# First MLP's y product three steps behind its h product in the first block, third buffer of g, scaled x in raw v's buffers

## Chip, cores, metric

The kernel runs on one core of a Trainium2 chip. The metric is the device time of one execution in microseconds (us). Before the change three runs gave 720.06, 719.28 and 715.47 us, so the median is 719.28 us; the profiled execution took 716.73 us, of which 715.0 us are the span between its first and last instruction.

## What is computed

Windowed attention (with a few global positions) over 2 batches, 8 heads, 768 tokens and 64 columns a head, then two MLPs on the 1536 tokens of 512 columns:

```python
x = attention(q, k, v, n_global, n_local)      # 1536 x 512
h = x @ w_in                                   # 512 -> 2048
x = (h * np.cos(h)) @ w_out                    # 2048 -> 512
g = x @ w_gate                                 # 512 -> 1536
silu = g * (1.0 / (1.0 + np.exp(-g)))
out = (silu * (x @ w_val)) @ w_out2            # 1536 -> 512
```

All operands are float32 (the weights come as wider words and are narrowed on the chip). Each float32 product is made of three matmuls: every operand is split into a rounded high part and a low rest, and high x high, high x low and low x high are summed.

## The kernel before

**Stages.** A prologue does the attention of tiles 0 to 3 (of 128 tokens each; there are 12). Then `first_mlp` walks through 48 steps: 3 blocks of 512 tokens times 16 column blocks j of w_in and w_out. A step s makes `h_mm(s)` (12 matmuls, h = x w_in, L274), the chain of cos on VectorE (DVE) and ScalarE (ACT), and `y_mm` (12 matmuls, y += g w_out, L350). Attention of tiles 4 to 11 is strewn over steps 0 to 30 by the table BASES. From step 32 on, and in `second_mlp`, the order is fixed by hand; before that the instructions of each engine are put in order by a list scheduler that takes the order of the code as priority and puts in the waits for buffers.

**The chain of a step.** `chain_a`: k (ACT, L300) from h. `chain_b`: f (DVE, L311), then sine and square on ACT (L320, L321). `chain_c`: h is overwritten in place by f times h (DVE, L328), and its high part goes into g (ACT, L332). `chain_d`: the low part of g (DVE, L338), which reads h for the last time. h lies in PSUM and has two buffers (pool `hp`, `bufs=2`), so h(s+2) can't start before `chain_d(s)` has ended. g has two buffers, y four PSUM banks, one per 128 output columns. ACT needs a table load when it goes from sine to the exponentials of the attention (L848) or back.

**Weights.** In the first block each w block is fetched (`get`), narrowed by three DVE instructions (`use`: L183, L186, L193) and split for its step (`prep_in`, `prep_out`: ACT L206, then DVE or GpSimd L210, by the tables WIE and WOE). Later blocks only split again.

**Order of the loop.** Step s of the first 32 does `h_mm(s)`, `y_mm(s - 2)`, `prep_in(s + 1)`, `chain_b(s - 1)`, attention, `chain_c(s - 1)`, `chain_d(s - 1)`, narrowing of w_in(s + 2) and w_out(s), `prep_out(s - 1)` and `chain_a(s)`.

**Buffers that the change touches.** Raw v is loaded by SP (L702) into two buffers `vr`; `v_scale_part` (L660) reads them in the prologue and `split_v` (L709 to L718) later. The attention output is scaled by `x_norm` into `xn` (L901, a buffer of its own) and transposed on TensorE (PE, L220). SP's queue holds loads and the DMA transposes pt<-ph (L865) in one order. The output of the last MLP leaves through tiles `osb` (L547, L549).

Of the kernel before, what the change touches and what calls it, by code (L numbers as in the profile page):

```python
# [22 lines left out]
P = 128  # L23
# [30 lines left out]
E4 = 2  # L54
LAG = 2
VB = 5
VBE = 7
# [12 lines left out]
def attention_moe_moe2_kernel(  # L70
# [175 lines left out]
    def first_mlp(c1, before, steps, last_block):  # L246
# [60 lines left out]
        def chain_f(s):  # L307
            n = BLOCKS[todo[s][0]][1]
            h, k = hs[s]
            f = ch_p.tile([P, 512], F32, tag="f", name="f")  # L310
            nc.vector.scalar_tensor_tensor(  # L311
                out=f[:, :n], in0=h[:, :n], scalar=INV2PI, in1=k[:, :n],
                op0=ALU.mult, op1=ALU.subtract,
            )
            fs[s] = f
# [49 lines left out]
        def begin():  # L365
            get("i", 0)
            get("i", 1)
            get("o", 0)
            use("i", w_in, 0)
# [4 lines left out]
        ch_p = c1.enter_context(tc.tile_pool(name="ch", bufs=2))  # L374
        g_p = c1.enter_context(tc.tile_pool(name="g", bufs=2))
        yp = c1.enter_context(tc.tile_pool(name="yp", bufs=4, space=PSUM))
        last = nsteps - NF1
        for s in range(last):
            early, late = steps.get(s, ((), ()))
            if s < NF1:  # L380
                get("i", s + 2)
                get("o", s + 1)
            ps = h_mm(s)
            if s >= 2:
                y_mm(s - 2)
# [8 lines left out]
            if s < NF1:  # L394
                use("i", w_in, s + 2)
                use("o", w_out, s)
            prep_out(s - 1)
            chain_a(s, ps)
# [50 lines left out]
    def second_mlp(c2, ch_p, g_p, hp, yp):  # L449
# [51 lines left out]
        def silu(s):  # L501
            n = BLOCKS[todo[s][0]][1]
            sl = ch_p.tile([P, 512], F32, tag="f", name="sl")
            nc.scalar.activation(out=sl[:, :n], in_=ps_.pop(("g", s))[:, :n], func=AF.Silu)  # L504
# [15 lines left out]
        def o_mm(s):  # L520
# [5 lines left out]
            for m in range(nt // P):  # L526
# [8 lines left out]
                if j == NF2 - 1:  # L535
                    end = b == len(BLOCKS) - 1
                    o = ch_p.tile([P, DM], F32, tag="kf"[end and m // 2], name="osb")
                    rows = slice(t0 + m * P, t0 + (m + 1) * P)
# [56 lines left out]
    def windowed_path():  # L595
# [7 lines left out]
        with ExitStack() as ca:  # L603
# [42 lines left out]
            pt_p = ca.enter_context(tc.tile_pool(name="pt", bufs=4, side="right"))  # L646
            xn_p = ca.enter_context(tc.tile_pool(name="xn", bufs=1, side="right"))
            sm_p = ca.enter_context(tc.tile_pool(name="sm", bufs=2, side="right"))
# [243 lines left out]
            def x_norm(i):  # L892
# [6 lines left out]
                nc.vector.tensor_tensor(out=r, in0=r, in1=vsc[b][:, H:2 * H], op=ALU.mult)  # L899
                xn = xn_p.tile([P, DM], F32, tag="xn", name="xn")  # L900
                nc.vector.tensor_tensor(  # L901
# [300 lines left out]
```

## Time and profile before

| | us |
|---|---|
| median of three runs | 719.28 |
| lowest, highest | 715.47, 720.06 |
| the profiled execution | 716.73 |
| its span | 715.0 |
| PE busy in the span | 662.3 (93%) |
| PE weight load busy | 521.5 (73%) |
| DVE busy | 483.9 (68%) |
| ACT busy | 394.7 (55%) |
| GpSimd busy | 115.3 (16%) |

The profile's times are us from the start of the span. Its shares are means over very different stages: from about 300 us on PE hardly waits, and in the first 200 us DVE is nearly as busy as PE. So each stage has to be read by itself.

### The profile page before, as it was taken

How to read it: one execution, taken by the hardware profiler on the slowest of the kernel's cores; microseconds unless marked ns; L12 is line 12 of the kernel's file. 1: busy time of each engine (PE TensorE's matmuls, PEld its weight loads, DVE VectorE, ACT ScalarE, POOL GpSimd, SP SyncE). 2: the span in 40 equal slices, each digit the busy share in tenths (PEclk: the TensorE clock that was granted, in tenths of full speed). 3: DMA queues.
4: the chain of work that ended last, by engine and by line, in shares of the span. 5: the costliest groups of instructions: out<-in, count | busy, mean ns of one | idle time of the engine just before them, and what ended most of it. 6: DMA issues, size and time to landing. Idle time of an engine off the chain costs nothing.

```text
span 715.0 us, 9068 instructions
## 1 busy us (share of the span) xinstructions
PE 662.3 (93%) x3276; PEld 521.5 (73%) x3276; DVE 483.9 (68%) x886; ACT 394.7 (55%) x820; POOL 115.3 (16%) x108
## 2 busy tenths in 40 slices
PE   4777898987898999999999999999999999999997
PEld 3345676756676777787888888888888888888885
DVE  4795999989987566747999869878443444433442
ACT  5566678777486898766666743332333333333331
POOL 2564333523322332420000000000000000000000
PEclk9996799998999999999999999999999999999999
DMA  6788546648534122300332224542000000100001
GB/s 222 190 195 211 170 132 224 172 130 201 136 104 68 37 49 45 60 1 30 102 104 89 88 59 126 161 126 88 30 30 0 1 1 0 60 0 1 1 0 63
DMA packets 69652, 62.73 MB, mean 88 GB/s; under 512 B 48896, under 2 KB 55296, under 8 KB 69600
## 3 DMA queue, kind: packets, MB, share of 16 engines
q1 hardware_dynamic: 69456, 61.95, 31.4%
q8 instruction: 27, 0.44, 0.2%
q14 instruction: 25, 0.20, 0.1%
q10 hardware_dynamic: 144, 0.13, 0.1%
HBM read 47.19 MB, written 3.15 MB: 70 GB/s over the span
## 4 chain that ended last, share of the span: by engine, by line
PE 65%; DVE 16%; ACT 10%; DMA 4%; issue 2%; POOL 1%; SPq 0%; DVEq 0%; ACTq 0%; POOLq 0%
PE v L492 14%; PE o L528 14%; PE g L492 14%; PE h L274 10%; PE y L350 10%; DMA pt<-ph 3%; ACT sb L848 3%; DVE w L193 2%; DVE w L186 2%; DVE sb L830 1%; PE s L778 1%; DVE w L183 1%; ACT L320 1%; ACT L848 1%; DVE h L328 1%
## 5 line engine op out<-in xcount | busy, mean ns | idle before, releaser
L210 DVE TENSOR_TENSOR ws<-w,ws 128x512 fp32r<-128x512 f32 x161 | 112.6, 720 | 95.1 <-ACT ws L206 94.9
L350 PE MATMUL y<-g,ws 128*128 128x512 f32 x576 | 145.8, 399 | 12.9 <-ACT g L332 11.4
L274 PE MATMUL h<-xh,ws 128*128 128x512 f32 (+1 forms) x392 | 136.3, 409 | 3.9 <-ACT xh L225 2.2
L350 PEld LDWEIGHTS y<-g,ws 128*128 128x128 f32 x576 | 109.1, 191 | 39.2 <-ACT g L332 10.9
L206 ACT CAST ws<-w 128x512 fp32r<-128x512 f32 x204 | 121.9, 615 | 21.1 <-DVE w L193 13.3
L528 PE MATMUL o<-ws,a 128*128 128x512 f32 x432 | 104.7, 391 | 0.0
L492 PE MATMUL v<-xh,ws 128*128 128x512 f32 x288 | 96.3, 395 | 0.0
L274 PEld LDWEIGHTS h<-xh,ws 128*128 128x128 f32 x392 | 77.4, 200 | 24.5 <-DVE g L338 3.6
L492 PE MATMUL g<-xh,ws 128*128 128x512 f32 x288 | 94.7, 390 | 0.0
L528 PEld LDWEIGHTS o<-ws,a 128*128 128x128 f32 x432 | 81.1, 188 | 18.4
L274 PE MATMUL h<-xl,ws 128*128 128x512 f32 (+1 forms) x196 | 78.8, 402 | 0.0
L210 POOL TENSOR_TENSOR ws<-w,ws 128x512 fp32r<-128x512 f32 x43 | 60.3, 1403 | 109.6 <-ACT ws L206 98.6
L504 ACT ACTIVATE sl<-g 128x512 f32<-128x512 f32 x36 | 21.5, 598 | 97.5 <-PE g L492 97.5
L492 PEld LDWEIGHTS v<-xh,ws 128*128 128x128 f32 x288 | 54.2, 188 | 12.7
L514 ACT CAST a<-sl 128x512 fp32r<-128x512 f32 x36 | 22.4, 622 | 72.6 <-DVE sl L510 72.6
L492 PEld LDWEIGHTS g<-xh,ws 128*128 128x128 f32 x288 | 54.1, 188 | 11.2
L492 PE MATMUL v<-xl,ws 128*128 128x512 f32 x144 | 56.9, 395 | 0.0
L492 PE MATMUL g<-xl,ws 128*128 128x512 f32 x144 | 56.0, 389 | 0.0
L193 DVE SCALAR_TENSOR_TENSOR w<-st,w 128x512 int32<-128x512 int32 x68 | 53.9, 802 | 0.8
L186 DVE SCALAR_TENSOR_TENSOR w<-st,w 128x512 int32<-128x512 int32 x68 | 48.6, 723 | 1.2
L300 ACT ACTIVATE k<-h 128x512 int32<-128x512 f32 x48 | 28.4, 592 | 34.4 <-PE h L274 34.3
L311 DVE SCALAR_TENSOR_TENSOR f<-h,k 128x512 f32<-128x512 f32 x48 | 32.9, 685 | 20.8 <-ACT k L300 20.5
(111 smaller groups left out, 821.9 us busy)
## 6 DMA issues: line engine op xcount, KB each, us to landing
st<-w1i SPq DMA_DIRECT2D x16, 512.0 KB, 3.8
st<-w1o SPq DMA_DIRECT2D x16, 512.0 KB, 4.3
st<-w2g SPq DMA_DIRECT2D x12, 512.0 KB, 3.7
st<-w2v SPq DMA_DIRECT2D x12, 512.0 KB, 3.7
st<-w2o SPq DMA_DIRECT2D x12, 512.0 KB, 3.7
vr<-v SPq DMA_DIRECT2D x16, 256.0 KB, 3.8
kr<-kT SPq DMA_DIRECT2D x12, 256.0 KB, 4.1
qr<-qT SPq DMA_DIRECT2D x12, 256.0 KB, 3.4
```

Of the source, the lines that this page charges most:

```text
L186: nc.vector.scalar_tensor_tensor(out=w, in0=hi, scalar=-(1 << 30), in1=w, op0=ALU.bitwise_and, op1=ALU.bitwise_or,)
L193: nc.vector.scalar_tensor_tensor(out=w, in0=lo, scalar=29, in1=w, op0=ALU.logical_shift_right, op1=ALU.bitwise_or,)
L206: nc.scalar.copy(out=s[:, 0, :], in_=w)
L210: e.tensor_tensor(out=s[:, 1, :], in0=w, in1=f32(s[:, 0, :]), op=ALU.subtract)
L274: nc.tensor.matmul(hps[s][:, c0:c1], lhsT=wis[s][:, a, k * P:(k + 1) * P], rhs=xx[:, k, t0 + c0:t0 + c1], start=(k == 0 and a == 0 and xx ...
L300: nc.scalar.activation(out=k[:, :n], in_=ps[:, :n], func=AF.Copy, scale=INV2PI)
L311: nc.vector.scalar_tensor_tensor(out=f[:, :n], in0=h[:, :n], scalar=INV2PI, in1=k[:, :n], op0=ALU.mult, op1=ALU.subtract,)
L350: nc.tensor.matmul(ys[b][m][:, :n], lhsT=w[:, a, m * P:(m + 1) * P], rhs=g[:, c, :n], start=(j == 0 and a == 0 and c == 0), stop=(j == NF1 ...
L492: nc.tensor.matmul(ps[:, :n], lhsT=w[:, a, k * P:(k + 1) * P], rhs=xx[:, k, t0:t0 + n], start=(k == 0 and a == 0 and xx is xh), stop=(k == ...
L514: nc.scalar.copy(out=a[:, 0, :n], in_=sl[:, :n])
L528: nc.tensor.matmul(os_[b][m], lhsT=a[:, c, m * P:(m + 1) * P], rhs=w[:, d, :], start=(j == 0 and c == 0 and d == 0), stop=(j == NF2 - 1 an ...
L848: nc.scalar.activation(out=a, in_=a, func=AF.Exp, bias=nm[:, h:h + 1], accum_out=sm[:, h:h + 1])
```

## The change

In the first 20 steps `y_mm` runs three steps behind `h_mm` instead of two; step 20 (`CATCH`) does two y products, and after it the distance is two again. The fetch, narrowing and split of w_out move one step later with it. g gets a third buffer. Room for it comes from f, which goes from two buffers to one, and from `xn`, which loses its own buffer and takes one of the two of `vr`. The second MLP's silu tile moves from f's buffers to k's, and three of the four output tiles of a block leave through g's buffers, the fourth through f's.

```diff
+CATCH = 20
-            f = ch_p.tile([P, 512], F32, tag="f", name="f")
+            f = ch_p.tile([P, 512], F32, tag="f", bufs=1, name="f")
...
-            get("o", 0)
...
-        g_p = c1.enter_context(tc.tile_pool(name="g", bufs=2))
+        g_p = c1.enter_context(tc.tile_pool(name="g", bufs=3))
...
                 get("i", s + 2)
-                get("o", s + 1)
+                get("o", s)
+            elif s == NF1:
+                get("o", s - 1)
             ps = h_mm(s)
-            if s >= 2:
+            if s <= CATCH:
+                if s >= 3:
+                    y_mm(s - 3)
+            if s >= CATCH:
                 y_mm(s - 2)
...
                 use("i", w_in, s + 2)
-                use("o", w_out, s)
-            prep_out(s - 1)
+                if s >= 1:
+                    use("o", w_out, s - 1)
+            elif s == NF1:
+                use("o", w_out, s - 1)
+            if s < CATCH:
+                prep_out(s - 2)
+            if s >= CATCH - 1:
+                prep_out(s - 1)
...
-            sl = ch_p.tile([P, 512], F32, tag="f", name="sl")
+            sl = ch_p.tile([P, 512], F32, tag="k", name="sl")
...
-                    o = ch_p.tile([P, DM], F32, tag="kf"[end and m // 2], name="osb")
+                    if m < 3:
+                        o = f32(g_p.tile([P, 2, DM], F32R, tag="g", name="osb")[:, 0, :])
+                    else:
+                        o = ch_p.tile([P, DM], F32, tag="f", bufs=1, name="osb")
...
-                xn = xn_p.tile([P, DM], F32, tag="xn", name="xn")
+                xn = vr_p.tile([P, DM], F32, tag="vr", name="xn")
```

The scheduler makes a new order of the first 250 us from this. Three places follow. Lines of the changed kernel are 1 higher near the top (L274 is L275) and 13 higher in the attention (L848 is L861).

PE, from the end of tile 6's attention product (x) to h of step 12. Before, the first four matmuls of y(10) (one for each of y's four banks, with g's high part) stand there:

```order
L888 MATMUL x_1780<-vs_1734,pt_1710 128x64
L350 MATMUL y_942<-g_1787,ws_1799 128x512
L350 MATMUL y_943<-g_1787,ws_1799 128x512
L350 MATMUL y_944<-g_1787,ws_1799 128x512
L350 MATMUL y_945<-g_1787,ws_1799 128x512
L274 MATMUL h_1836<-xh_106,ws_1773 128x512
L274 MATMUL h_1836<-xl_107,ws_1773 128x512
```

In the changed kernel the whole of y(9) and two transposes stand there:

```order
L901 MATMUL x_1756<-vs_1710,pt_1686 128x64
L351 MATMUL y_981<-g_1690,ws_1775 128x512 x3
L351 MATMUL y_982<-g_1690,ws_1775 128x512 x3
L351 MATMUL y_983<-g_1690,ws_1775 128x512 x3
L351 MATMUL y_984<-g_1690,ws_1775 128x512 x3
L221 MATMUL xT_1877<-ident_124,xn_1875 128x128 x2
L275 MATMUL h_1812<-xh_106,ws_1749 128x512
```

So y(10) has gone behind h(12), and what stands ahead of h(12) is a product of the step before it.

ACT, at the first exponentials of tile 8, around step 14. Before, these stand after the sine of step 14, all behind one table load:

```order
L225 CAST xh_106<-xT_2101 128x4x128
L332 CAST g_2144<-h_2037 128x512
L848 ACT_TABLE_LOAD
L848 ACTIVATE sb_1977,sum_1973<-sb_1977,nm_1972 128x256 x2
L848 ACTIVATE sb_2075,sum_1973<-sb_2075,nm_1972 128x256 x2
L300 ACTIVATE k_2155<-h_2110 128x512
```

In the changed kernel the sine of step 14 (f_2116) stands between two of them:

```order
L226 CAST xh_106<-xT_2077 128x4x128
L861 ACT_TABLE_LOAD
L861 ACTIVATE sb_1953,sum_1949<-sb_1953,nm_1948 128x256 x2
L321 ACT_TABLE_LOAD
L321 ACTIVATE f_2116<-f_2116 128x512
L861 ACT_TABLE_LOAD
L861 ACTIVATE sb_2051,sum_1949<-sb_2051,nm_1948 128x256
```

There are two table loads more here, and 25 instead of 23 in the whole program.

SP's queue in the prologue, at the transposes of tile 2. Before, the loads of raw v of the second batch (vr_666, vr_671 are its last two) stand behind them:

```order
L865 DMA_TRANSPOSE pt_594<-ph_591 128x8x128
L865 DMA_TRANSPOSE pt_599<-ph_596 128x8x128
L702 DMA vr_666<-v 128x512
L702 DMA vr_671<-v 128x512
L110 DMA kr_76<-kT 128x4x128
L865 DMA_TRANSPOSE pt_688<-ph_685 128x8x128
```

In the changed kernel one load (vr_577) stands between these transposes, and two more ahead of the first of tile 3 (pt_683):

```order
L878 DMA_TRANSPOSE pt_589<-ph_586 128x8x128
L715 DMA vr_577<-v 128x512
L878 DMA_TRANSPOSE pt_594<-ph_591 128x8x128
L111 DMA kr_76<-kT 128x4x128
L715 DMA vr_661<-v 128x512
L715 DMA vr_666<-v 128x512
L878 DMA_TRANSPOSE pt_683<-ph_680 128x8x128
```

A load has moved into the queue ahead of transposes, and its buffer is one that the transposed xn of tile 1 has held.

## Rows read from the trace of the kernel before

**Rows 1.** Page, the clock granted to PE in 40 slices, tenths of full speed

```profile
PEclk9996799998999999999999999999999999999999
```

**Rows 2.** Windows: stretch, length, busy time of each engine, clock, DMA share, GB/s

```profile
60.00:120.00 60.00, 50.23 (x286) 36.97 (x286) 54.25 (x109) 44.24 (x94) 18.70 (x14) 0.87 0.63 181
120.00:180.00 60.00, 51.73 (x268) 39.50 (x268) 54.07 (x112) 46.48 (x106) 23.99 (x20) 0.90 0.65 172
180.00:240.00 60.00, 55.00 (x324) 42.21 (x324) 46.12 (x103) 42.97 (x94) 17.24 (x13) 1.00 0.37 88
240.00:300.00 60.00, 57.95 (x374) 44.72 (x374) 41.55 (x89) 51.37 (x109) 21.00 (x17) 1.00 0.28 54
406.00:715.00 309.00, 303.64 (x1322) 248.07 (x1320) 163.36 (x259) 107.72 (x193) 0.00 (x0) 1.00 0.14 44
```

**Rows 3.** Waits, 60 to 300 us, PE's: total us, times, longest

```profile
PE y L350 <- ACT g L332: 11.4, 7, 4.2
PE x L888 <- DMA pt<-ph: 4.6, 3, 2.4
PE s L755 <- DVE xn L901: 3.3, 2, 2.9
PE h L274 <- DVE g L338: 1.6, 2, 1.1
```

**Rows 4.** Timeline at y(4) and h(6): start, duration, engine, instruction, idle before

```profile
117.98 1.49 PE L350 MATMUL y<-g,ws 128*128 128x512 f32 x4 [3.10 <-ACT g L332]
118.18 0.68 DVE L338 TENSOR_TENSOR g<-h,g 128x512 fp32r<-128x512 f32 x1
119.26 0.63 PE L274 MATMUL h<-xh,ws 128*128 128x512 f32 x1
```

**Rows 5.** Timeline at y(10) and h(12)

```profile
172.06 2.08 PE L350 MATMUL y<-g,ws 128*128 128x512 f32 x4 [4.25 <-ACT g L332]
172.51 0.68 DVE L338 TENSOR_TENSOR g<-h,g 128x512 fp32r<-128x512 f32 x1
173.94 0.63 PE L274 MATMUL h<-xh,ws 128*128 128x512 f32 x1
```

**Rows 6.** Groups of DVE instructions of the weights, 60 to 200 us: busy, mean ns

```profile
L193 DVE SCALAR_TENSOR_TENSOR w<-st,w 128x512 int32<-128x512 int32 x27 | 25.7, 975 | 0.0
L186 DVE SCALAR_TENSOR_TENSOR w<-st,w 128x512 int32<-128x512 int32 x27 | 19.3, 737 | 0.0
L183 DVE TENSOR_SCALAR w<-st 128x512 int32<-128x512 int32 x28 | 15.3, 576 | 3.5 <-DMA st<-w1i 3.5
L210 DVE TENSOR_TENSOR ws<-w,ws 128x512 fp32r<-128x512 f32 x11 | 9.6, 870 | 0.5 <-ACT ws L206 0.4
```

**Rows 7.** Chain that ended last, one whole y product at full clock

```profile
296.36 2.72 PE y L350 x12
```

**Rows 8.** Timeline of ACT around a table load

```profile
108.59 0.62 ACT L206 CAST ws<-w 128x512 fp32r<-128x512 f32 x1 [2.31 <-DVE nm L838]
109.23 1.28 ACT L848 ACT_TABLE_LOAD   x1
110.52 0.51 ACT L848 ACTIVATE sb<-sb,nm 128x256 f32<-128x256 f32 x1
```

**Rows 9.** Page, DMA issues: KB each, us from issue to landing

```profile
vr<-v SPq DMA_DIRECT2D x16, 256.0 KB, 3.8
```

**Rows 10.** Timelines of the prologue: raw v, its absolute value, xT of tile 1, exponentials

```profile
39.96 2.34 SPq L702 DMA_DIRECT2D vr<-v  x2
47.83 0.63 ACT L660 ACTIVATE va<-vr 128x512 fp32r<-128x512 f32 x1 [1.00 <-PE vsum L661]
50.40 0.64 PE L220 MATMUL xT<-ident,xn 128*128 128x128 f32 x4
54.37 0.47 ACT L810 ACTIVATE sb<-s,nm 128x256 f32<-128x256 f32 x1 [1.93 <-DVE nm L800]
```

**Rows 11.** Timeline of the end

```profile
704.01 5.63 PE L528 MATMUL o<-ws,a 128*128 128x512 f32 x24
709.00 0.69 DVE L547 COPY osb<-o 128x512 f32<-128x512 f32 x1 [0.67 <-PE o L528]
709.68 0.42 DVE L541 COPY osb<-o 128x256 f32<-128x256 f32 x1
710.59 0.37 ACTq L544 DMA_DIRECT2D out<-osb  x1
```

More of the change, by code (lines that the diff above doesn't have):

```diff
@@ L646, in windowed_path @@
             pt_p = ca.enter_context(tc.tile_pool(name="pt", bufs=4, side="right"))
-            xn_p = ca.enter_context(tc.tile_pool(name="xn", bufs=1, side="right"))
             sm_p = ca.enter_context(tc.tile_pool(name="sm", bufs=2, side="right"))
```

## The prediction

> **What bounds the kernel now.** I read the windows first, because one share for the whole span says little here. They show where PE can gain at all [rows 2]: from 406 us to the end it is busy 303.64 of 309 us, and the order of its instructions is the same there before and after the change. Nothing is to be had there. Between 60 and 300 us PE is busy 50.23, 51.73, 55.00 and 57.95 of 60 us, so 25.1 us are idle. In the first two of these windows DVE is busier than PE: 54.25 and 54.07 of 60, that is 90%.
>
> The waits of PE come next [rows 3]. The largest is the one that the change speaks of: y's first matmul waits for g's high part, 11.4 us in 7 places. Waits for transposed probabilities (4.6) and for xn (3.3) follow, and h waiting for g's low part has only 1.6. Read alone, this says that y should go one step later.
>
> Then I looked into the timeline at the two longest of the seven, which hold 3.10 and 4.25 of the 11.4 us [rows 4, 5]. The reader should look at what stands behind y on PE: h(s+2), whose PSUM buffer is free only when chain_d(s) has read h(s) for the last time. At y(4) that instruction ends at 118.18 + 0.68 = 118.86, and h(6) starts at 119.26. At y(10) it ends at 173.19, and h(12) starts at 173.94. So h would have waited for the same chain, 0.40 and 0.75 us less long than it did. The chain h, k, f, sine, square, h, g on ACT and DVE is what is late, and y only stands first in the row of those that wait. h keeps its two buffers, so the chain keeps its rate.
>
> **The change part by part.** The sum is made against the profiled execution, 716.73 us, of which 715.0 are the span.
>
> *y behind h.* Where y's first four matmuls stood ahead of h and waited, they now stand behind it, and h starts as soon as its own buffer is free. Gain: 0.40 + 0.75 = 1.15 [rows 4, 5]; for the five shorter waits I take nothing. Between 0 (the chain itself moves) and 11.4 us (all waits vanish and h never takes their place [rows 3]), I take **-1.2**.
>
> *w_out one step later.* In the 16 steps of the first block one w_out less has been narrowed and split by DVE at any time: 0.576 + 0.737 + 0.975 us for the narrowing, and for the split 0.87 us where DVE does it, about every second time early on [rows 6], in sum 2.7 us. This work doesn't vanish, it lies behind step 15, where DVE has room (46.12 of 60 [rows 2]). In the stage that it leaves DVE is 90% busy; with 90% of it on the path it brings **-2.4** (between 0 and -2.7). Its DMA also goes a step later in SP's queue, with no one waiting for it.
>
> *Two y products in step 20.* One y product, 12 matmuls of 2.72 us together [rows 7], leaves steps 3 to 19 and comes back in step 20. Ahead of it PE can come to an h up to 2.72 us earlier wherever PE and not the chain was late; at step 20 it pays that back, with 120 - 112.95 = 7.05 us of idle PE between 180 and 300 us to pay from [rows 2]. I take **0**, between -2.7 and +2.7.
>
> *Third g buffer, one f buffer.* f is written by DVE (L311) and last read by DVE (L328), in that order for successive steps, so one buffer adds no wait on DVE. No wait of g for a y product is among the waits, so the third buffer frees nothing by itself; it only lets y be later. **0**.
>
> *Order on ACT.* The new order has two more table loads, at step 14. Each takes 1.28 us, and the next activation starts at once after it, 109.23 + 1.28 = 110.51 against 110.52 [rows 8]. Two are 2.56 us. Between 180 and 240 us ACT is busy 42.97 of 60, between 240 and 300 us 51.37 [rows 2]; the chain needs it. I take half, **+1.3**, between 0 and 2.6.
>
> The Trainium skill, ScalarE: Activation LUTs, section on what ACT_TABLE_LOAD costs, gives 1283 ns for the load, as here, and 1380 ns more for a drain, 2.66 us in all. The trace shows no drain: the cast ahead ends at 109.21 and the load starts at 109.23 [rows 8]. By the page the two would be an estimated 5.3 us and my half 2.7.
>
> *xn in vr's buffers.* Now a load of raw v must wait for transposes of xn, and xn for the last reader of raw v. In the prologue vr_577 can't be issued before xT of tile 1 has ended at 51.04; before the change two such loads went out between 39.96 and 42.30 [rows 10]. With 3.8 us to land [rows 9] it is there at 54.8, and ACT's order has its absolute value, 0.63 us, ahead of the exponentials that started at 54.37. They would start at 55.5, 1.1 us later. Behind that load in SP's queue stands one transpose of tile 2, and behind ACT's wait stand the exponentials of tile 3. Against that, ACT's later reads of raw v no longer stand where they stood. I take half, **+0.5**, between 0 and, if the same happens again at each of a few later loads, the 7.9 us that PE's waits for pt and xn amount to now [rows 3].
>
> *The end.* The third output tile of the last block takes the buffer of g that the last product reads, so its copy on DVE waits for that product's end. Now it starts at 709.00, while the product runs to 704.01 + 5.63 = 709.64; then it would take 0.69 us, and the half tile behind it on DVE (now from 709.68), ACT's half and the last DMA (now at 710.59) follow that much later [rows 11]. **+0.7**, nothing hides it. At the ends of the other two blocks the same wait costs nothing, since PE goes on with g and v products and isn't waiting for that copy.
>
> Sum: -1.2 - 2.4 + 0 + 0 + 1.3 + 0.5 + 0.7 = -1.1 us, so 715.6 for an execution like the profiled one. That one lay 2.55 us under the median of the three runs; the mean of the four times is 717.9. I put the forecast on that mean: 717.9 - 1.1 = **716.8 us**.
>
> **Rivals.**
> *The waits really go* (faster). If a late chain were a matter of PE's order, with h(s+2) no longer bound to chain_d(s) after the shift, the 11.4 us of y's waits go, and the end costs 0.7: 716.73 - 11.4 + 0.7 = 706.0 us. For it: the granted clock is 0.87 and 0.90 in the two windows where most of the waits lie and 1.00 after [rows 1, 2], so the idle time costs more than itself, and h at the lower clock is longer. Against it: h(6) and h(12) start within 0.75 us of the end of their chains. Chance 0.18. The Trainium skill, TensorE: Matmul & The Clock Gate, in its part on oscillation, tells the same of waits that come again and again: PE is throttled after each, and work that goes on without such gaps runs at the full clock. The trace agrees so far that the lower clock falls in the windows with the most idle time.
>
> *v loads block SP's queue* (slower). A load whose buffer is held by xn stands at the head of SP's queue with the transposes of the next probabilities behind it; x waits for these, and xn for x. From the point on where such a load stands there longer than the 3.8 us of its landing, PE's waits for pt and xn double: 716.73 + 7.9 + 1.1 + 0.7 = 726.4 us. For it: after the change, loads stand between transposes in the queue. Against it: in the steps, a v load is issued four steps ahead of its split. Chance 0.13.
>
> *It does not do what it says.* At h(12) y(9) stands ahead of h, not y(8): the scheduler has undone one step of the distance. If the shift brings nothing and its costs stay: 716.73 + 1.3 + 0.5 + 0.7 = 719.2 us. Chance 0.17.
>
> **How the numbers follow.** The sum as worked out has 0.52. Its own range, with the bounds of w_out, step 20, ACT and the sharing and some 2 us for the scatter between runs (715.47 to 720.06), is 712 to 722. For 8 in 10 the range goes towards both rivals: **709 to 724**. One per cent, 7.2 us, is about what a measurement of this kernel can tell from no change. Within it lie the sum and the case without effect, 0.69; faster 0.18; slower 0.13.
>
> **What would show it.** PE's wait of y for g falls below 3 us and that of h for g's low part rises to 6 us or more; if both are small, the first rival holds. PE's idle time between 60 and 300 us stays between 20 and 28 us, and DVE's share from 60 to 180 us near 90%. h(12) starts within 1 us of the end of chain_d(10). The last DMA goes out about 0.9 us after the last product's end now and 1.6 us then. Waits of PE for pt or xn above 12 us would show the second rival. My prediction is wrong if the chain itself becomes shorter because DVE or ACT gets other instructions ahead of it.

## The result, and the profile after

| | before | after |
|---|---|---|
| median, us | 717.96 (715.47 to 720.06, 4 runs) | 707.63 (707.17 to 708.74, 4 runs) |
| the profiled execution | 716.73, span 715.0 | 708.01, span 705.8 |
| ratio after to before | | 0.9874, 95% interval 0.9851 to 0.9896 |

The change saves 1.3%. The forecast was 716.8 us and its range 709.0 to 724.0, so the time lies 9 us under the one and 1.4 us under the other.

The windows of the changed kernel, with the columns of [rows 2]:

```profile
60.00:120.00 60.00, 51.16 (x286) 38.39 (x287) 55.11 (x120) 49.16 (x101) 21.00 (x17) 0.89 0.73 201
120.00:180.00 60.00, 53.74 (x323) 40.52 (x322) 55.30 (x112) 43.06 (x100) 21.88 (x19) 0.94 0.58 155
180.00:240.00 60.00, 55.08 (x284) 42.29 (x284) 44.92 (x105) 50.70 (x107) 18.30 (x15) 1.00 0.38 92
240.00:300.00 60.00, 57.85 (x389) 45.82 (x386) 38.52 (x80) 48.92 (x103) 20.62 (x16) 1.00 0.24 46
396.80:705.80 309.00, 302.72 (x1318) 247.32 (x1316) 163.38 (x259) 107.08 (x191) 0.00 (x0) 1.00 0.13 43
```

They differ little from [rows 2]. PE is idle for 240 - 51.16 - 53.74 - 55.08 - 57.85 = 22.2 us between 60 and 300 us, where it was 25.1, and DVE is as busy as before. Equal windows hide the gain, because the same 60 us now hold later steps. The waits of PE between 60 and 300 us, to lay beside [rows 3]:

```profile
PE h L275 <- DVE g L339: 6.9, 6, 1.7
PE y L351 <- DVE ws L211: 3.6, 2, 2.6
PE s L768 <- DVE xn L914: 2.7, 2, 1.9
PE y L351 <- ACT ws L207: 2.1, 3, 1.1
PE x L901 <- DMA pt<-ph: 1.9, 2, 1.2
PE y L351 <- ACT g L333: 1.1, 2, 0.9
```

y's wait for g fell from 11.4 to 1.1 us, h's wait for the chain rose from 1.6 to 6.9, and y now also waits for the split of w_out (3.6 + 2.1). The first two the prediction had said; the wait for the split it had not.

To see where the time went, one needs the same event in both kernels, not the same moment. I take `chain_a`'s k<-h on ACT, of which there is one per step. Steps 4, 6 and 8 of the kernel before:

```profile
103.96 0.61 ACT L300 ACTIVATE k<-h 128x512 int32<-128x512 f32 x1
...
123.54 0.60 ACT L300 ACTIVATE k<-h 128x512 int32<-128x512 f32 x1 [0.63 <-PE h L274]
...
140.38 0.57 ACT L300 ACTIVATE k<-h 128x512 int32<-128x512 f32 x1
```

The same steps of the changed kernel:

```profile
101.12 0.58 ACT L301 ACTIVATE k<-h 128x512 int32<-128x512 f32 x1
...
114.22 0.58 ACT L301 ACTIVATE k<-h 128x512 int32<-128x512 f32 x1
...
129.67 0.58 ACT L301 ACTIVATE k<-h 128x512 int32<-128x512 f32 x1
```

From k(4) to k(8) it took 36.42 us and takes 28.55. The table does this for the whole span and for every kernel of this study: the start of k(0), the lengths of four groups of steps, and the stretch from k(31) to the end of the span. All are differences of such rows in the profiled executions. A profiled execution is one run, not the median of its kernel: that of e1 lies 1.8 us above its median, those of e3, e4 and e8 lie 2.7, 2.4 and 4.0 us below theirs.

| profiled kernel | k(0) at | steps 0-4 | 4-8 | 8-17 | 17-31 | k(31) to end | span |
|---|---|---|---|---|---|---|---|
| before | 75.32 | 28.63 | 36.42 | 78.30 | 96.07 | 400.25 | 715.0 |
| before, again (e5) | 73.33 | 28.21 | 36.79 | 77.53 | 99.02 | 400.41 | 715.3 |
| changed | 71.64 | 29.48 | 28.55 | 79.68 | 95.30 | 401.15 | 705.8 |
| e1 sharing alone | 71.47 | 25.15 | 37.22 | 76.59 | 97.61 | 400.56 | 708.6 |
| e2 buffers, old loop | 70.57 | 27.14 | 38.15 | 75.71 | 98.91 | 401.32 | 711.8 |
| e3 y late, w_out early | 70.84 | 27.63 | 37.64 | 76.70 | 96.33 | 401.36 | 710.5 |
| e4 y early, w_out late | 71.56 | 28.73 | 36.16 | 77.46 | 99.17 | 401.42 | 714.5 |
| e6 sharing, three buffers | 77.32 | 26.53 | 38.38 | 75.50 | 97.36 | 400.51 | 715.6 |
| e7 changed, own xn | 73.73 | 30.15 | 30.22 | 79.82 | 95.22 | 401.36 | 710.5 |
| e8 w_out late alone | 73.32 | 33.78 | 38.07 | 77.65 | 96.01 | 400.56 | 719.4 |
| e9 v loaded later | 74.68 | 25.78 | 37.20 | 75.98 | 97.55 | 400.52 | 711.7 |
| e10 changed, tail undone | 72.96 | 29.57 | 29.48 | 78.24 | 95.27 | 400.19 | 705.7 |
| e11 changed, catch at 28 | 71.14 | 29.48 | 29.39 | 78.60 | 96.74 | 401.26 | 706.6 |
| e12 v split on POOL | 73.45 | 28.15 | 40.41 | 73.73 | 97.59 | 400.37 | 713.7 |
| e13 changed, v on POOL | 68.03 | 32.85 | 30.19 | 80.45 | 95.30 | 400.67 | 707.5 |

Against the mean of the two profiles of before, the changed kernel gains 2.7 us ahead of k(0) and 8.1 in steps 4 to 8, loses 1.1 and 1.8 in the groups beside these, gains 2.2 in steps 17 to 31, and loses 0.8 at the end. What happens in steps 4 to 8 is seen in one window, k(4) to k(8). Before:

```profile
103.96:140.38 36.42, 32.03 (x186) 24.47 (x185) 34.69 (x75) 28.65 (x62) 15.44 (x11) 0.95 0.66 185
```

After:

```profile
101.12:129.67 28.55, 26.33 (x168) 19.59 (x166) 27.97 (x59) 25.78 (x57) 13.11 (x10) 1.00 0.62 178
```

DVE is busy 34.69 of 36.42 and 27.97 of 28.55 us: it sets the pace in both, and after the change it has 16 instructions less to do between the same two points. Which ones the groups of DVE in this stretch tell. Before (busy us, mean ns):

```profile
L193 DVE SCALAR_TENSOR_TENSOR w<-st,w 128x512 int32<-128x512 int32 x10 | 9.0, 912 | 0.0
L186 DVE SCALAR_TENSOR_TENSOR w<-st,w 128x512 int32<-128x512 int32 x10 | 7.1, 726 | 0.0
L183 DVE TENSOR_SCALAR w<-st 128x512 int32<-128x512 int32 x9 | 3.6, 417 | 1.0 <-DMA st<-w1i 1.0
```

After:

```profile
L187 DVE SCALAR_TENSOR_TENSOR w<-st,w 128x512 int32<-128x512 int32 x7 | 4.9, 720 | 0.0
L194 DVE SCALAR_TENSOR_TENSOR w<-st,w 128x512 int32<-128x512 int32 x7 | 4.6, 680 | 0.0
L184 DVE TENSOR_SCALAR w<-st 128x512 int32<-128x512 int32 x6 | 4.5, 793 | 0.3 <-DMA st<-w1i 0.3
```

Seven weights are narrowed in these four steps instead of ten: 19.7 us of DVE became 14.0. The clock granted to PE in the stretch rose from 0.95 to 1.00, and its matmuls fell from 186 to 168; ACT's busy time fell from 28.65 to 25.78 us. So other work than the narrowing left these steps as well.

Not all of this is work put off. A weight takes three narrowing instructions, and the 32 weights take 96. Counted from the start of the span, 60 of them stand before k(8) in both profiles of before and 57 in the changed kernel; before k(4) it is 33 and 38. So by k(8) one weight less has been narrowed, and the rest of the difference between k(4) and k(8) was done earlier, ahead of k(4). In sum DVE is busy for 106.9 us up to k(8), where it was 113.7 and 112.0.

### The profile page after: what moved, and what is told of

It reads as the page before. It is cut to its first block, busy times and chain, and to the rows that moved or that the text cites. A ratio compares the mean times of both kernels' runs of the same rounds, so it can differ in the third digit from the quotient of the medians.

```text
span 705.8 us, 9077 instructions
## 1 busy us (share of the span) xinstructions
PE 656.9 (93%) x3276; PEld 517.7 (73%) x3276; DVE 479.5 (68%) x886; ACT 398.0 (56%) x822; POOL 112.6 (16%) x108
## 4 chain that ended last, share of the span: by engine, by line
PE 68%; DVE 14%; ACT 9%; DMA 5%; issue 2%; POOL 1%; SPq 0%; DVEq 0%; POOLq 0%; ACTq 0%
PE v L503 14%; PE o L539 14%; PE g L503 14%; PE h L275 11%; PE y L351 10%; DMA pt<-ph 2%; ACT sb L861 2%; DMA st<-w1i 2%; DVE w L194 2%; DVE w L187 2%; PE s L791 2%; DVE sb L843 1%; DVE ws L211 1%; DVE w L184 1%; PE s L768 1%
## 5 line engine op out<-in xcount | busy, mean ns | idle before, releaser
L211 DVE TENSOR_TENSOR ws<-w,ws 128x512 fp32r<-128x512 f32 x161 | 113.7, 727 | 98.5 <-ACT ws L207 98.4
L275 PE MATMUL h<-xh,ws 128*128 128x512 f32 (+1 forms) x392 | 132.2, 399 | 7.0 <-DVE g L339 6.9
L275 PEld LDWEIGHTS h<-xh,ws 128*128 128x128 f32 x392 | 75.2, 193 | 27.1 <-DVE g L339 9.9
L275 PE MATMUL h<-xl,ws 128*128 128x512 f32 (+1 forms) x196 | 77.0, 393 | 0.0
L211 POOL TENSOR_TENSOR ws<-w,ws 128x512 fp32r<-128x512 f32 x43 | 57.7, 1344 | 119.7 <-ACT ws L207 113.8
L187 DVE SCALAR_TENSOR_TENSOR w<-st,w 128x512 int32<-128x512 int32 x68 | 50.1, 747 | 1.2
L194 DVE SCALAR_TENSOR_TENSOR w<-st,w 128x512 int32<-128x512 int32 x68 | 49.6, 739 | 0.8
L329 DVE SCALAR_TENSOR_TENSOR h<-f,h 128x512 f32<-128x512 f32 x48 | 33.1, 690 | 21.4 <-ACT f L322 21.4
L301 ACT ACTIVATE k<-h 128x512 int32<-128x512 f32 x48 | 28.4, 591 | 29.9 <-PE h L275 29.8
```

The source lines that it names most:

```text
L187: nc.vector.scalar_tensor_tensor(out=w, in0=hi, scalar=-(1 << 30), in1=w, op0=ALU.bitwise_and, op1=ALU.bitwise_or,)
L194: nc.vector.scalar_tensor_tensor(out=w, in0=lo, scalar=29, in1=w, op0=ALU.logical_shift_right, op1=ALU.bitwise_or,)
L211: e.tensor_tensor(out=s[:, 1, :], in0=w, in1=f32(s[:, 0, :]), op=ALU.subtract)
L275: nc.tensor.matmul(hps[s][:, c0:c1], lhsT=wis[s][:, a, k * P:(k + 1) * P], rhs=xx[:, k, t0 + c0:t0 + c1], start=(k == 0 and a == 0 and xx ...
L301: nc.scalar.activation(out=k[:, :n], in_=ps[:, :n], func=AF.Copy, scale=INV2PI)
L329: nc.vector.scalar_tensor_tensor(out=h[:, :n], in0=f[:, :n], scalar=0.5, in1=h[:, :n], op0=ALU.subtract, op1=ALU.mult,)
```

## The experiments

All ratios are to the kernel before in the same comparison (its medians lay between 716.88 and 717.86 us).

| | median, us | ratio, 95% interval |
|---|---|---|
| e1 sharing alone | 708.62 | 0.9875 (0.9836 to 0.9913) |
| e2 buffers, old loop | 713.54 | 0.9953 (0.9921 to 0.9984) |
| e3 y late, w_out early | 715.10 | 0.9963 (0.9938 to 0.9988) |
| e4 y early, w_out late | 718.62 | 1.0019 (0.9994 to 1.0044) |
| e5 before again | 717.07 | one run |
| e6 sharing, three buffers | 718.82 | 1.0022 (0.9984 to 1.0060) |
| e7 changed, own xn | 713.63 | 0.9953 (0.9927 to 0.9978) |
| e8 w_out late alone | 725.26 | 1.0121 (1.0065 to 1.0178) |
| e9 v loaded later | 714.55 | 0.9960 (0.9944 to 0.9976) |
| e10 changed, tail undone | 707.85 | 0.9861 (0.9835 to 0.9888) |
| e11 changed, catch at 28 | 708.74 | 0.9882 (0.9857 to 0.9907) |
| e12 v split on POOL | 715.66 | 0.9969 (0.9953 to 0.9984) |
| e13 changed, v on POOL | 709.53 | 0.9880 (0.9854 to 0.9905) |

My first theory was that the gain ahead of k(0) comes from the sharing, and the gain in the steps from the later y and the relief of DVE by w_out; the rival was that the sharing has no part in it.

**e1, sharing alone.** The kernel before with two edits:

```diff
-            xn_p = ca.enter_context(tc.tile_pool(name="xn", bufs=1, side="right"))
...
-                xn = xn_p.tile([P, DM], F32, tag="xn", name="xn")
+                xn = vr_p.tile([P, DM], F32, tag="vr", name="xn")
```

> The kernel before with one edit: scaled x takes raw v's buffers. In the changed kernel h(0) starts 3.8 us earlier than before, h(6) 8.7 us, and the end 9.2 us. Theory P (the sharing gives the part ahead of h(0)): h(0) 3 to 4 us earlier, the steps as before, 714 us. Theory L (all comes from the later y and w_out; the part ahead of h(0) from w_out 0 no longer loaded and narrowed there): h(0) within 0.5 us of before, 718 us. My recorded term for this edit was +0.5 us: 718.5 us.

708.6 us: neither theory. This edit alone gives nearly the whole gain of the change. The table shows it by another road: 2.9 us ahead of k(0), 3.3 in steps 0 to 4, nothing in steps 4 to 8 and 1.3 in steps 8 to 17. ACT's order has changed too: it has 19 table loads instead of 23, three instead of five both in steps 0 to 4 and in steps 4 to 8.

**e2, the buffers without the later y and w_out.** The changed kernel with the loop of before (`y_mm(s - 2)` throughout, `get("o", 0)` in `begin`, `get("o", s + 1)`, `use("o", w_out, s)`, `prep_out(s - 1)`):

```diff
-            if s <= CATCH:
-                if s >= 3:
-                    y_mm(s - 3)
-            if s >= CATCH:
+            if s >= 2:
                 y_mm(s - 2)
```

> The changed kernel with the loop of the kernel before: y two steps behind h, w_out loaded, narrowed and split when it was; all buffers as changed (third g, one f, xn in vr, output tiles in g). Theory P: the part ahead of h(0) is kept, 3.8 us, the steps as before, 0.7 to 0.9 us lost at the end: 715 us. Theory L: nothing is left but the end's loss, 718.5 us. If the buffers were the whole gain: 708 us.

713.5 us, near theory P's 715, but 4.9 us slower than e1: the third g, the single f and the output tiles in g, which I had put at nothing but the end's 0.7, take more than half of the sharing's gain away again. The order of e2 has 23 table loads again, as before; which of these edits does it was not tried. The end costs 0.8 of it (401.32 against 400.56); steps 0 to 4 take 2.0 us longer than in e1 and steps 17 to 31 take 1.3 longer.

**e3 and e4, one half of the shift each.** e3 is the changed kernel with w_out loaded (the first one in `begin`), narrowed and split as early as before, y three steps late. e4 has y two steps behind, w_out loaded and narrowed one step later:

```diff
 (e3)
-                get("o", s)
+                get("o", s + 1)
...
-                if s >= 1:
-                    use("o", w_out, s - 1)
+                use("o", w_out, s)
...
-            if s < CATCH:
-                prep_out(s - 2)
-            if s >= CATCH - 1:
-                prep_out(s - 1)
+            prep_out(s - 1)
 (e4)
-            if s <= CATCH:
-                if s >= 3:
-                    y_mm(s - 3)
-            if s >= CATCH:
+            if s >= 2:
                 y_mm(s - 2)
...
-            if s < CATCH:
-                prep_out(s - 2)
-            if s >= CATCH - 1:
-                prep_out(s - 1)
+            prep_out(s - 1)
```

> The changed kernel with w_out loaded, narrowed and split in the steps in which it was before, y three steps behind h. Theory Y (the distance of y itself brings the gain in the steps): within 1 us of the changed kernel, 708 us. Theory W (DVE's relief by one w_out less at any time brings it): the gain in the steps, about 5 us, is lost: 713 us, 711 if my recorded 2.4 us for it was right.

> The changed kernel with y two steps behind h throughout, w_out loaded and narrowed one step later as changed (its split in the same step, where y needs it next). Theory W: 708 to 710 us. Theory Y: the gain in the steps is lost, 713 us, and PE's wait of y for g is again 8 to 11 us between 60 and 300 us.

With e2 and the changed kernel this is a square: neither 713.5, y late 715.1, w_out late 718.6, both 707.6 us. Neither theory Y nor W holds. w_out late alone costs 5 us; y late alone gains nothing (the 1.6 us that it lies above e2 can't be told from scatter, and its order has 27 table loads, four more than e2's, so it isn't the distance of y alone); both together gain 6 us. Steps 4 to 8 show where the halves fail: 38.15, 37.64 and 36.16 us without one or the other, 28.55 with both. The narrowing does too: before k(8) stand 60, 60 and 61 of its instructions in e2, e3 and e4, and 57 in all five kernels that have both. In e3 PE's wait of y for g is still there between 60 and 300 us:

```profile
PE y L351 <- ACT g L333: 6.9, 6, 2.3
```

y is later in the program but not in time. The split of w_out(s - 1) needs one of two buffers, and y(s - 3) reads it; with the split as early as before, y(s - 3) has to be out of the way as early as before. (That this is what holds it is read from the code and the wait, it was not tried with a third buffer.) In e4 y's waits for g are back (9.0 us between 60 and 300 us, as theory Y had it), the weights are wanted as early as before, and DVE narrows about ten of them between k(4) and k(8):

```profile
L187 DVE SCALAR_TENSOR_TENSOR w<-st,w 128x512 int32<-128x512 int32 x10 | 7.0, 716 | 0.0
```

**e8, w_out later alone, all buffers as before.** The kernel before with

```diff
-            get("o", 0)
...
-                get("o", s + 1)
+                get("o", s)
...
-                use("o", w_out, s)
+                if s >= 1:
+                    use("o", w_out, s - 1)
+            elif s == NF1:
+                use("o", w_out, s - 1)
```

> The kernel before with w_out loaded and narrowed one step later, split in the step in which it is narrowed; y two steps behind h, all buffers as before. By my recorded term 716.9 - 2.4 = 714.5 us. By the pair with and without this among kernels with the changed buffers (718.6 against 713.5) it costs 5 us: 722 us, with PE's y waiting for the split of w_out or ACT standing in front of it.

725.3 us, a loss of 8 where my term for this part was a gain of 2.4. Steps 0 to 4 take 33.78 us instead of 28.4. Moved later in the program without its reader, the narrowing isn't put off: 62 of its instructions stand before k(8), where 60 stood. I read this as the same deadline with less time.

**e5, before again; e6, sharing with three buffers.** e5 has no edit. e6 is e1 with one more:

```diff
-            vr_p = ca.enter_context(tc.tile_pool(name="vr", bufs=2, side="right"))
+            vr_p = ca.enter_context(tc.tile_pool(name="vr", bufs=3, side="right"))
```

> The kernel before, unchanged, profiled a second time. In the first profile PE's four s products from 16.85 us take 0.29 us each, in all five profiles with sharing 0.18 us from 17.5 us on, although the instructions ahead of them are the same in the same order. Theory C (chance of the clock: the half-rate stretch from 16.85 us is a property of that execution): here the first xn starts near 34.8 us instead of 36.53 and h(0) some 1.7 us earlier, with the rest of the time unchanged. Theory P (the part ahead of h(0) is the sharing's): xn at 36.5 and the first k at 75.3 us again.

> The kernel before with scaled x in raw v's pool, but with three buffers there instead of two, so that as much room is there as before the change. Theory P1 (the shortage, loads of v held back by xn, brings the gain): 716 to 717 us. Theory P2 (the other order that comes with one pool brings it, the shortage nothing): 708 to 710 us, as with sharing alone (708.6).

e5 has k(0) at 73.33 us instead of 75.32 with the same instructions, and the span is 0.3 us longer: theory C holds for about 2 us ahead of k(0), and these 2 us don't reach the end (17 to 31: 99.02 against 96.07). So a part of what one profile shows at the start is chance. A part isn't: in the eight profiles with two shared buffers k(0) lies between 68.0 and 73.0 us, in the six with xn apart between 73.3 and 75.3, on the mean 71.0 against 74.0. The clock granted to PE differs between these executions (from 35 to 65 us 0.94 in e13, which has the earliest k(0), and 0.61 in e10, which has the latest of the eight), so I compare those with 0.71 to 0.77: k(0) lies between 70.6 and 71.6 in five with two shared buffers (changed, e1, e2, e4, e11) and between 73.3 and 74.7 in four with xn apart (e7, e8, e9, e12). With three shared buffers it is 77.3, at a granted clock of 0.60, and the median of the total is 718.8 us, with the widest scatter of all (713.7 to 723.6). So P1 comes out within 2 us of its number: without the shortage there is no gain.

**e7, the change without the sharing.** Room for xn's own buffer comes from k:

```diff
+            xn_p = ca.enter_context(tc.tile_pool(name="xn", bufs=1, side="right"))
...
-            k = ch_p.tile([P, 512], I32, tag="k", name="k")
+            k = ch_p.tile([P, 512], I32, tag="k", bufs=1, name="k")
...
-            sl = ch_p.tile([P, 512], F32, tag="k", name="sl")
+            sl = ch_p.tile([P, 512], F32, tag="kf"[s % 2], bufs=1, name="sl")
```

> The changed kernel with a buffer of its own for scaled x again; the room comes from k, which has one buffer instead of two (the next k is written after f has read the last). If the later y and w_out gain by themselves and the sharing by itself: 707.6 + 4 = 712 us. If the later y and w_out gain nothing without the sharing: 718 us, with the end's 0.9 us. If the sharing gives nothing here: 708 us.

713.6 us. So the later y and w_out do gain without the sharing, 3.4 us, and the sharing gains 6 on top of them (8.3 alone, so the two don't add up: 3.4 + 8.3 would be 11.7, and it is 9 to 10). The 6 us include whatever the lost buffer of k costs e7, which was not tried alone. Between k(4) and k(8) e7 looks like the changed kernel:

```profile
103.88:134.10 30.22, 27.86 (x173) 20.88 (x172) 27.94 (x65) 27.67 (x60) 12.88 (x9) 1.00 0.63 162
```

Here DVE has 27.94 us of work, as in the changed kernel, where e1 has 36.70 in 37.23:

```profile
96.61:133.84 37.23, 33.15 (x190) 25.52 (x188) 36.70 (x81) 26.53 (x62) 14.96 (x11) 0.91 0.66 185
```

The short steps 4 to 8 (28.6 to 30.2 us in all five kernels with y and w_out both late, 36.2 to 40.4 in all ten others) are thus the work of the shift. The sharing counts at the start, where the changed kernel is 2.1 us ahead of e7; alone it also counts in steps 0 to 4.

**e9 and e12, what the sharing does in the steps.** The second block's v come in tiles 4, 5, 6 and so on, each split into two halves. In the order of DVE's instructions before, tile 4's halves stand ahead of f(0), tile 5's between f(0) and f(1), tile 6's between f(4) and f(5). With sharing alone tile 4's stand behind f(0), tile 5's second half behind f(4), tile 6's behind f(5) and f(7). The second theory: v's preparation is held back out of steps that DVE limits. e9 gets the same places in the kernel before by another means, xn keeping its buffer. e12 takes tile 4's halves off DVE, upon which tile 6's stand behind f(5). (The two expectations speak of the first v of the block where the halves that matter are those of tiles 5 and 6.)

```diff
 (e9)
-                add(0, E, load_v, i)
+                add(2, E, load_v, i)
 (e12)
-VLE = "DGGGDDDGDDGD"
+VLE = "DGGGGDDGDDGD"
-VHE = "DDDDDDDDGDDD"
+VHE = "DDDDGDDDGDDD"
```

> The kernel before with one edit: each raw v of the steps is loaded one step later in the program (the last step's half, two half steps later); xn keeps its own buffer. In the order the split of the first v of the second block then stands behind f of step 4, as it does with sharing alone, where before it stood behind f of step 0. Theory V (sharing gains because v's preparation is held back out of steps 0 to 4, where DVE sets the pace): 709 to 712 us, and DVE has spent some 3 us less on v before k of step 6. Theory S (it is the sharing itself, through the part ahead of h(0)): 716 to 717 us. If holding it back costs, because x waits for v: 720 us.

> The kernel before with one edit: the two halves of the first v of the second block are made on POOL (both were on DVE); buffers, loads, y and w_out as before. The order up to the first steps stays that of before. In both profiles of before, the two of this v on DVE stand ahead of f(5), and from k(4) to k(6) it takes 20.0 and 19.6 us; in the kernels where v is held back 16.0 to 16.5. Theory V (the split ahead of f(5) is what lengthens these two steps): k(4) to k(6) in 16 to 17 us, the start as before, and of the 3.5 us up to 4 come back in steps 6 to 10, as with the later load: 713 to 716 us. Theory S (nothing without the sharing): 717 us and 19.6 to 20 us from k(4) to k(6).

e9: 714.6 us, 2.9 us faster by the ratio, more than nothing and less than 709 to 712. Its steps 0 to 4 take 25.78 us, like e1's 25.15: the later place of v in the program is enough to give those steps their gain. Its k(0) is at 74.68, without e1's 2.9 us at the start. That the gain is v's work out of DVE's way, as the theory says, isn't shown. DVE's work on v and on the row maxima of the attention between k(0) and k(4), before:

```profile
L717 DVE CAST vs<-vr 128x512 f16<-128x512 f32 x1 | 0.4, 415 | 0.0
L718 DVE TENSOR_TENSOR vs<-vr,vs 128x512 f16<-128x512 f32 x1 | 0.7, 686 | 0.0
L830 DVE CUSTOM_DVE_ANT_0 sb<-s,m 128x256 f32<-128x256 f32 x8 | 3.0, 415 | 0.0
```

And in e9:

```profile
L717 DVE CAST vs<-vr 128x512 f16<-128x512 f32 x2 | 1.6, 838 | 0.0
L718 DVE TENSOR_TENSOR vs<-vr,vs 128x512 f16<-128x512 f32 x1 | 0.7, 677 | 0.0
L830 DVE CUSTOM_DVE_ANT_0 sb<-s,m 128x256 f32<-128x256 f32 x6 | 2.3, 414 | 0.0
```

DVE is busy 24.85 us there instead of 27.97, but v takes more of it and not less, because tile 4's halves have come in behind f(0); what has gone is other work, two of eight row maxima for one. Like e1, e9 has 19 table loads instead of 23, which is 4 x 1.28 = 5.1 us of ACT. e6 and e12, with 21, have three in steps 0 to 4 and five in steps 4 to 8, and neither reaches k(8) earlier than the kernel before does. So fewer table loads are a rival that no run separates from DVE's order. e12 hit its numbers, 715.7 us (2.2 us faster by the ratio), and from k(4) to k(6) 15.94:

```profile
101.60 0.61 ACT L300 ACTIVATE k<-h 128x512 int32<-128x512 f32 x1
...
117.54 0.57 ACT L300 ACTIVATE k<-h 128x512 int32<-128x512 f32 x1
...
142.01 0.57 ACT L300 ACTIVATE k<-h 128x512 int32<-128x512 f32 x1
```

But from k(6) to k(8) it takes 24.47 us, where before had 16.84: it saves 3.6 us and gives back 7.6, and only steps 8 to 17 bring some of this in again. Taking one v off DVE moves the long step, it doesn't shorten the stage as much.

**e10, e11 and e13, the rest of the change.** e10 gives the third output tile of the last block a buffer of k; e11 sets `CATCH = 28`; e13 is e10 with the edit of e12.

```diff
 (e10, e13)
+                    if end and m == 2:
+                        o = ch_p.tile([P, DM], F32, tag="k", name="osb")
-                    if m < 3:
+                    elif m < 3:
 (e11)
-CATCH = 20
+CATCH = 28
```

> The changed kernel with one edit: the third output tile of the last block goes to a buffer of k, which is free, instead of the buffer of g that the last product reads. The profile of the changed kernel shows 0.9 us less gain at the end than at h(31); with the edit that stays: 706.7 us, and the last DMA goes out 0.9 us after the last product's end instead of 1.8. If the copy was not what is late there: 707.6 us.

> The changed kernel with the catching up of y in step 28 instead of 20, and w_out's split later up to there. In the changed kernel's profile the lead over before falls by 1.5 us between steps 20 and 25. Theory G (PE is the bound from step 22 on, so the y product is paid wherever it stands): 707.6 us, within 1 us. Theory D (the two y in step 20 cost because they meet the chain there): 706 us. If y's later end in the first block or the longer tail of the shift costs: 709 us.

> The changed kernel with the same edit (both halves of the first v of the second block on POOL) and the third output tile of the last block in a buffer of k. Theory V says that the changed kernel already has the gain, since its split stands behind f(5): 706.7 us from the tail alone, k(4) to k(6) in 13 us as there. If DVE is still what sets the pace in steps 0 to 10, its 1.6 us less bring 705 us. If POOL then comes too late with its other splits: 709 us.

The end of the changed kernel, where the copy of the third tile waits for the last product (compare [rows 11]):

```profile
693.88 5.63 PE L539 MATMUL o<-ws,a 128*128 128x512 f32 x24
...
699.56 0.69 DVE L561 COPY osb<-o 128x512 f32<-128x512 f32 x1 [1.35 <-PE o L539]
...
701.06 0.37 ACTq L558 DMA_DIRECT2D out<-osb  x1
```

The same end in e10:

```profile
696.82 3.56 PE L539 MATMUL o<-ws,a 128*128 128x512 f32 x15
...
699.74 0.69 DVE L563 COPY osb<-o 128x512 f32<-128x512 f32 x1 [0.67 <-PE o L539]
...
701.28 0.38 ACTq L560 DMA_DIRECT2D out<-osb  x1
```

The product ends at 699.51 and the last DMA goes out 1.55 us later; in e10 it ends at 700.38 and the DMA goes out 0.90 us later. In the table e10 has 400.19 us from k(31) to the end, e13 with the same edit 400.67, and the six kernels with the changed output tiles 401.15 to 401.42. So 0.65 us are there by the last DMA and 0.5 to 1.2 by the table, but that is too small for the median: 707.85 us (704.71 to 709.01, 5 runs) can't be told from 707.63. e11 is 1.1 us above the changed kernel, with intervals that overlap: this agrees with theory G, that the y product is paid wherever it stands. e13 is no gain on the changed kernel either (709.5, near the branch of its expectation in which POOL comes too late): k(0) is the earliest of all at 68.03, but steps 0 to 4 take 32.85 us instead of 29.48, and steps 4 to 8 take 30.19, where nothing was left to take. So no version was found that is faster than the changed kernel by more than can be measured; e1, with one edit, comes within 1 us of it.

## Why the prediction was wrong, step by step

**The step that failed: xn in vr's buffers.** The prediction priced it at +0.5 us, between 0 and 7.9, all on the side of loss, because a shared buffer only adds waits. Alone it measures -8.3 us (e1), on top of the rest -6.0 (707.6 against 713.6 in e7). The waits are real, and where the prediction followed one it was about right: in the changed kernel loads of raw v wait for xT, here between 10 and 72 us,

```profile
SPq L715 <- PE xT L221: 2.9, 2, 2.5
```

one of them leaves at 49.97, right behind xT of tile 1 that ends at 49.94, and the exponentials that started at 54.37 (53.01 in e5) start at 54.97, 0.6 us (2.0) later where 1.1 had been worked out. The loads have also changed places in the queue. In the kernel before two of them leave at 23.20 us,

```profile
23.20 1.57 SPq L702 DMA_DIRECT2D vr<-v  x2
```

and in e1 they leave behind the four transposes that follow:

```profile
37.82 1.05 SPq L701 DMA_DIRECT2D vr<-v  x2
```

What was missed is that a program whose order is made from its dependences comes out in another order when they change, and that the other order can be the shorter one. For steps 0 to 4, e9 shows that a later load of v is enough (25.8 us, where it was 28.2 and 28.6); DVE is busy for nearly the whole of these steps in either, and whether its order or the fewer table loads on ACT make them shorter stays open. For the start, some 3 us, the runs show only that it comes with two shared buffers (eight profiles) and not with three (one) or with xn apart (six); which instruction's place does it stays open. In e6 steps 0 to 4 are short as well, 26.53 us, though tile 5's halves stand ahead of f(1) as before, and the gain is lost at the start, k(0) at 77.32.

**y behind h (-1.2) and w_out one step later (-2.4).** The waits moved as forecast, 11.4 to 1.1 and 1.6 to 6.9 us, and the reading behind it was right: the chain is late, not y. But the two were priced apart and added. e3, e4 and e8 show that neither gains alone (+1.6, which is within scatter, +5.1 and +8.3 us) and that both together bring 6 to 8 us in steps 4 to 8. The prediction's "the chain keeps its rate" failed there: four steps take 28.55 us instead of 36.42 with the same two buffers of h. The count of the relief was right, one w_out less by k(8) (57 narrowing instructions instead of 60), but it comes only where y is late too, and DVE's busy time up to k(8) falls by 5 to 7 us in the changed kernel (by 3 to 5 in e7, without the sharing) and not by 2.7; why by so much stays open. In steps 8 to 17 the work comes back, 39 narrowing instructions instead of 36, and these steps take 1.8 us longer. In total, without the sharing, the shift brings -3.4 us (e7), where the terms -1.2 - 2.4 + 1.3 + 0.7 make -1.6.

**Two y in step 20 (0).** Right: e11 changes nothing that can be measured.

**Third g buffer, one f buffer (0).** No wait for these buffers is among the waits of e2, but with them and the other output tiles it is 4.9 us slower than e1, of which 0.8 is the end. I take the rest for order, not a wait; it was not taken apart.

**Two more table loads (+1.3).** They are there (25 on ACT instead of 23). All five kernels with y and w_out both late have seven in steps 8 to 17 instead of five, and these steps take 78.3 to 80.5 us there and 73.7 to 78.3 in the ten others. A cost of the size of the term is possible, then, but the one w_out more lies in the same steps, and no run takes the loads away alone.

**The end (+0.7).** Right: the copy starts 0.05 us behind the product's end instead of 0.64 ahead of it, and the DMA goes out 1.55 us after the end instead of 0.95, 0.6 us more; in the table the end costs 0.8.

**h(12) within 1 us of the chain.** Wrong in its detail. chain_d(10) and h(12) of the changed kernel:

```profile
162.33 0.68 DVE L339 TENSOR_TENSOR g<-h,g 128x512 fp32r<-128x512 f32 x1
...
160.66 3.89 PE L351 MATMUL y<-g,ws 128*128 128x512 f32 x10 [2.57 <-DVE ws L211]
...
164.53 0.48 PE L275 MATMUL h<-xh,ws 128*128 128x512 f32 x1
```

The chain ends at 163.01, and h(12) starts 1.52 us later, because a y that had itself waited 2.57 us for the split of its weight stands ahead of it. The later w_out put a new wait there that the prediction didn't name.

**The rivals.** "The waits really go" gave 706.0 us, next to the result, but not by its mechanism: h took over 6.9 us of the waits, PE's idle time fell by 3 us and not by 11, and e1 gets the same time with 7.7 us of y's waits for g left:

```profile
PE y L350 <- ACT g L332: 7.7, 8, 2.4
```

"v loads block SP's queue" is refuted: PE's waits for pt and xn fell (4.6 and 3.3 to 1.9 and 2.7). The last sentence of the prediction named what came in steps 4 to 8: the chain became shorter where DVE had other, and less, work ahead of it. It had no term and no chance of its own, and so the range ended at 709.

## What to carry to other kernels

Where a scheduler makes the order, an edit of a buffer is an edit of the order: its price can have either sign, and a range that counts only waits is one-sided. Compare such kernels by the time of the same event (one instruction per step), not by equal windows; a gain that windows of 60 us hide stands out at once. When work is to be moved out of a stage that one engine limits, move its reader with it: here the producer moved alone was not put off, and lost 8 us.

## What the hardware showed that I had not expected

The same instructions in the same order ran at two speeds in two executions. The first s and vsum products of the second tile, before:

```profile
16.85 1.23 PE L778 MATMUL s<-kr,qr 64*128 64x256 f32 x4
18.01 0.79 PE L661 MATMUL vsum<-va,onesr 128*128 128x512 f32 x1
18.73 1.23 PE L778 MATMUL s<-kr,qr 64*128 64x256 f32 x4
```

And before again (e5):

```profile
16.83 1.22 PE L778 MATMUL s<-kr,qr 64*128 64x256 f32 x4
17.98 0.56 PE L661 MATMUL vsum<-va,onesr 128*128 128x512 f32 x1
18.48 0.70 PE L778 MATMUL s<-kr,qr 64*128 64x256 f32 x4
```

Four products take 1.23 us in the one and 0.70 in the other, after the same work. I read this as TensorE at the lower of its two levels in the first and at the higher in the second; the granted clock stands at 1.00 in the records of both for this stretch, so only the durations say so. k(0) then lies 1.99 us apart, and nothing of it is left at the end (span 715.0 and 715.3). The Trainium skill, TensorE: Matmul & The Clock Gate, Part 1, says that the chip's watch over the activity runs freely and doesn't start with the kernel; two executions that begin the same and speed up at different times agree with that. For the reader of one profile it means that a difference of 2 us at some step, as here, need not be the edit's; it was the eight profiles against six, and the medians, that told the sharing's part from chance.
